# Moving the tail operand and one float32r table to other SBUF addresses in a Fourier-transform and MLP kernel

## The chip, the cores and the metric

The kernel runs on one core of one Trainium2 chip. The metric is device time in microseconds (us) of one execution. Times come from three executions; one further execution was taken with the hardware profiler, and all rows below are from that one.

## The reference

What has to be computed is the real part of a two-dimensional Fourier transform of each of four 3008 x 256 blocks, and then a two-layer perceptron with the SiLU function on the 12032 rows that come out:

```python
batch, seq, dim = (4, 3008, 256)
n_tokens, d_model, d_ff = (12032, 256, 2048)
X = np.fft.fft(x, axis=1)
X = np.fft.fft(X, axis=2)
x = X.real.reshape(B * S, D)
h = x @ w_in
g = h * (1.0 / (1.0 + np.exp(-h)))
return g @ w_out
```

## The kernel before

**Work in chunks.** The transform along the sequence is folded by symmetry until 1506 columns per block are left, in four classes of 376, 378, 376 and 376 columns (`CLASS`, L40). All columns of the four blocks are worked off in 13 chunks (`CHUNKS`, L42): the four classes of block 0 singly, with 376 or 378 columns, then nine chunks of 502 columns. A chunk takes 16 steps, one for each 128 of the 2048 hidden columns.

**A step.** `first` (L443) issues six matmuls, L449 to L451 twice each: the weights `abh` and `abl` (transform along the model axis and `w_in` in one, split into a float32r part and the rest of it) against the chunk's spectrum `uv`, also split. `act` (L459) forms the two signs on VectorE and the SiLU on ScalarE. `second` (L497), three steps later (`LAG`), issues twelve matmuls, four each of L512, L513 and L519, with `w_out` as `woh` and `wol` against the activations `gh` and `gl`, into four accumulators. So a step is 18 matmuls, each with a weight load of 128 x 128 just ahead of it. All these operands are float32r.

**A transform.** Twelve or so steps apart a step also carries the transform of one class of the next block. `turns` (L778 to L784) fixes by hand where: for blocks 1 to 3, with j = 3b + 1, class 0 in chunk j - 1, class 1 in chunk j - 1 too, class 2 in chunk j at step 8, class 3 in chunk j + 1 at step 4. `operand` (L250) prepares `xf` (float32, two buffers in turn) on VectorE, and from the last third of it the tail operand `xh` (float32r, one buffer, L331). `transform` (L339) then issues matmuls on TensorE, with `xf` and `xh` as the stationary operand and the tables as the moving one. For classes 0, 2 and 3 this is twice the same row of seven:

- the tails: one of 376 (or 380) columns (L348) and two of 188 (or 190) columns (L351), `xh` against a float32r table;
- the main part: four of 188 (or 190) columns (L354), `xf` against a float32 table.

Class 0 takes its tables from `t2f` and `t2r`, class 2 from `tef` and `ter`, class 3 from `tof` and `tor`; class 1 uses `tz`, `ter`, `tor`, `tef` and `tof` in 19 matmuls. So class 0 and class 3 issue the same shapes in the same order, and differ by where their operands lie. Behind the transform come the six matmuls of the next step's `first`.

**Addresses.** A pool takes the next free address, and pools lie behind each other in the order in which they are opened: `wts`, `fold`, `raws`, `xs` (with `xf`, `xh` and `wide`), `cp` (`uv`, `ub`), `gh`, `gl`, `mp`, and behind them `wr`, which is closed after the weights are loaded, and in its place `tabs` with the tables (`load_tables`, L615). `place` (L65) puts an empty tile of so many bytes ahead of the next one and thereby moves all that follows.

Of the kernel before, what the change touches and what calls it, by code (L numbers as in the profile page):

```python
# [24 lines left out]
F32 = mybir.dt.float32  # L25
F32R = mybir.dt.float32r
# [24 lines left out]
def fft_mlp(ctx, tc, x1, x2, x2_first, w_in, w_out, te_f, te_r, to_f, to_r, tz_r, t2_f, t2_r, t2f, rot1, rot2, dft, minus_eye, out):  # L51
# [8 lines left out]
    xs = ctx.enter_context(tc.tile_pool(name="xs", bufs=1))  # L60
    cp = ctx.enter_context(tc.tile_pool(name="cp", bufs=3))
# [3 lines left out]
    def place(pool, name, shift):  # L65

        pool.tile([128, shift // 4], F32, name="before_" + name, bufs=1)
# [25 lines left out]
    tabs = {}  # L93
# [461 lines left out]
    late, wr_stack = ctx.enter_context(ExitStack()), ctx.enter_context(ExitStack())  # L555
    wr = wr_stack.enter_context(tc.tile_pool(name="wr", bufs=1))
    ps = late.enter_context(tc.tile_pool(name="ps", bufs=4, space=PSUM))
    place(cp, "uv", 480)
    once = cp.tile([128, 2048], F32, tag="uv", name="once")
    sign, dft_0, dft_1 = once[:, 1790:1792], once[:, 1792:2048], once[:, 0:256]  # L560
    dft_sb = [t.rearrange("p (m k) -> p m k", m=2) for t in (dft_0, dft_1)]
# [53 lines left out]
    def load_tables(q):  # L615
        wr_stack.close()
        pool = ctx.enter_context(tc.tile_pool(name="tabs", bufs=1))
        for name, pair in (("te", (te_f, te_r)), ("to", (to_f, to_r))):
            tabs[name] = [pool.tile([128, t.shape[-1]], d, name=name + x) for t, d, x in zip(pair, (F32, F32R), "fr")]
            for dst, t in zip(tabs[name], pair):  # L620
                nc.gpsimd.dma_start(out=dst, in_=t)
            if name == "te":
                tabs["tz"] = pool.tile([128, 378], F32R, name="tz")
                nc.gpsimd.dma_start(out=tabs["tz"], in_=tz_r)
        tabs["t2"] = pool.tile([128, 376], F32, name="t2f"), wts.tile([128, 1128], F32R, tag="t2", name="t2r")[:, :752]
        for dst, t in zip(tabs["t2"], (t2_f, t2_r)):
            nc.gpsimd.dma_start(out=dst, in_=t)
# [41 lines left out]
    xf = xs.tile([128, 1280], F32, tag="xf", name="xf", bufs=2)  # L669
# [150 lines left out]
    for q, n, m in ((1, 1, 2), (2, 2, 3), (3, 3, 4), (4, 4, 5), (5, 7, 10), (6, 11, 12), (7, 11, 12)):  # L820
        after.setdefault(n - 1 if q < 5 else n, []).append((upper_wo, q))
        fills.setdefault(n + 1, []).append((lower_wo, q))
        if q >= FULL // 2:
            if q > 2:
                fills.setdefault(n - 2 if q == 3 else n - 1, []).append((clear_wo, q))
            mids.setdefault(n + 1, []).append((high_wo, q))
            lows.setdefault(m, []).append((low_wo, q))
    lows[5].append((load_tables, 4))
    after.setdefault(8, []).append((load_wo, 7))
    pace = wts.tile([1, 2], F32, name="pace")  # L830
# [178 lines left out]
```

## Time and profile before

| | |
|---|---|
| median of three executions | 860.05 us (859.88 to 860.71) |
| the profiled execution | 860.15 us |
| its span, first to last instruction | 858.4 us |
| TensorE matmuls busy | 850.9 us, 99% of the span |
| TensorE weight loads busy | 742.7 us, 87% |
| VectorE busy | 719.2 us, 84% |
| ScalarE busy | 511.8 us, 60% |
| GpSimd busy | 167.5 us, 20% |

Matmuls are pipelined, and their ends are modelled: the duration of one is longer than the distance from its start to the next one's, so the distance is what counts. A matmul's busy time alone tells nothing of its speed.

### The profile page before, as it was taken

Reading aid. Unit: us, or ns where it says so; the run is one execution under the profiler, and the core shown is the slowest. Engines: PE = TensorE matmul, PEld = TensorE weight load, DVE = VectorE, ACT = ScalarE, POOL = GpSimd, SP = SyncE. Lnnn points to the kernel's source line nnn. Section 1 sums busy time; section 2 is a strip of 40 time slices with the busy share of each in tenths; the row PEclk is TensorE's granted clock in tenths of the full one; section 3 lists DMA queues with packets and bytes.
Section 4 is the critical chain, followed back from the end, with each engine's and each line's share of the span. In section 5 each row is a group of like instructions: output and inputs, shape, how many; then the busy total and the mean of one; then the engine's idle time right before and its main releaser. Section 6 shows DMA issues by size and latency. Waiting matters only on the chain.

```text
span 858.4 us, 11009 instructions
## 1 busy us (share of the span) xinstructions
PE 850.9 (99%) x4066; PEld 742.7 (87%) x4066; DVE 719.2 (84%) x1074; ACT 511.8 (60%) x648; POOL 167.5 (20%) x239
## 2 busy tenths in 40 slices
PE   8999999999999999999999999999999999999998
PEld 6799999999988888888888888888888888888886
DVE  5899999999898987989789978889878887777773
ACT  5767856565656565566565556457656556545454
POOL 4757541323040401305013000502000000000000
PEclk9999999999999999999999999999999999999999
DMA  9755454073341516035034203404021011201001
GB/s 322 265 152 78 111 82 89 2 122 32 53 93 5 103 49 105 4 21 135 1 59 97 11 1 56 100 0 58 1 10 48 4 7 49 10 1 49 1 0 49
DMA packets 24182, 52.12 MB, mean 61 GB/s; under 512 B 3728, under 2 KB 13072, under 8 KB 24128
## 3 DMA queue, kind: packets, MB, share of 16 engines
q1 hardware_dynamic: 19888, 38.21, 21.2%
q0 software_dynamic: 4240, 13.21, 8.6%
q8 instruction: 32, 0.52, 0.3%
q14 instruction: 22, 0.18, 0.1%
HBM read 36.17 MB, written 12.34 MB: 57 GB/s over the span
## 4 chain that ended last, share of the span: by engine, by line
PE 97%; DMA 2%; DVE 0%; ACT 0%; SPq 0%; issue 0%; ACTq 0%
PE acc L513 20%; PE acc L519 20%; PE acc L512 20%; PE pq L449 10%; PE pq L451 10%; PE pq L450 10%; PE pq L354 3%; DMA win<-in_w_in_dram 2%; PE pq L351 1%; PE acc L510 1%; PE pq L348 1%; ACT wf L82 0%; PE pq L676 0%; PE pw L588 0%; DVE wf L86 0%; SPq L78 0%
## 5 line engine op out<-in xcount | busy, mean ns | idle before, releaser
L480 ACT ACTIVATE h<-h 128x1004 f32<-128x1004 f32 (+3 forms) x208 | 202.5, 974 | 281.5 <-DVE h L465 278.5
L513 PE MATMUL acc<-g,wol 128*128 128x502 f32 (+2 forms) x824 | 307.5, 373 | 0.0
L512 PE MATMUL acc<-g,woh 128*128 128x502 f32 (+2 forms) x824 | 307.2, 373 | 0.0
L495 DVE TENSOR_TENSOR g<-h,g 128x1004 fp32r<-128x1004 f32 (+3 forms) x208 | 240.8, 1159 | 14.1 <-ACT g L483 13.0
L519 PE MATMUL acc<-g,woh 128*128 128x502 f32 (+2 forms) x824 | 213.5, 373 | 0.0
L483 ACT ACTIVATE g<-h 128x1004 fp32r<-128x1004 f32 (+3 forms) x208 | 202.7, 975 | 7.2 <-PE acc L513 0.9
L463 DVE SCALAR_TENSOR_TENSOR p<-ub,a,pq 128x502 f32<-128x502 f32 (+2 forms) x208 | 144.7, 695 | 73.4 <-PE pq L451 69.7
L513 PEld LDWEIGHTS acc<-g,wol 128*128 128x128 f32 x824 | 155.6, 189 | 22.1
L512 PEld LDWEIGHTS acc<-g,woh 128*128 128x128 f32 x824 | 155.7, 189 | 21.8
L519 PEld LDWEIGHTS acc<-g,woh 128*128 128x128 f32 x824 | 153.1, 189 | 21.8
L449 PE MATMUL pq<-uv,abh 128*128 128x502 f32 (+2 forms) x416 | 158.0, 380 | 0.0
L451 PE MATMUL pq<-uv,abl 128*128 128x502 f32 (+2 forms) x416 | 155.1, 373 | 0.0
L450 PE MATMUL pq<-uv,abh 128*128 128x502 f32 (+2 forms) x416 | 154.9, 372 | 0.0
L464 DVE TENSOR_TENSOR h<-p,pq 128x502 f32<-128x502 f32 (+2 forms) x208 | 132.8, 638 | 22.1 <-DVE p L463 0.5
L465 DVE TENSOR_TENSOR h<-p,pq 128x502 f32<-128x502 f32 (+2 forms) x208 | 131.2, 631 | 0.0
L449 PEld LDWEIGHTS pq<-uv,abh 128*128 128x128 f32 x416 | 78.6, 189 | 11.2 <-issue 0.2
L451 PEld LDWEIGHTS pq<-uv,abl 128*128 128x128 f32 x416 | 78.5, 189 | 10.9
L450 PEld LDWEIGHTS pq<-uv,abh 128*128 128x128 f32 x416 | 78.6, 189 | 10.6
L150 POOL DMA_DIRECT2D raw<-in_x_dram x22 | 19.1, 882 | 222.1 <-DMA raw<-in_x_dram 221.0
L234 POOL TENSOR_TENSOR ri<-ri,raw 128x256 f32<-128x256 f32 x24 | 22.7, 953 | 135.4 <-ACT ri L229 134.9
L528 ACT ACTIVATE o<-acc 128x502 f32<-128x502 f32 (+2 forms) x52 | 28.0, 558 | 16.4 <-PE acc L519 14.0
L218 POOL TENSOR_TENSOR raw<-raw 128x512 f32<-128x512 f32 x12 | 16.2, 1348 | 18.5 <-DMA raw<-in_x_dram 18.5
(140 smaller groups left out, 471.2 us busy)
## 6 DMA issues: line engine op xcount, KB each, us to landing
raw<-in_x_dram SPq DMA_DIRECT2D x22, 512.0 KB, 8.4
raw<-in_x_dram POOLq DMA_DIRECT2D x20, 512.0 KB, 7.4
out_dram<-o SPq DMA_DIRECT2D x36, 251.0 KB, 2.1
win<-in_w_in_dram SPq DMA_DIRECT2D x8, 512.0 KB, 8.5
wo<-in_w_out_dram SPq DMA_DIRECT2D x8, 512.0 KB, 8.8
out_dram<-o SPq DMA_DIRECT2D x12, 188.0 KB, 4.2
ub<-wide SPq DMA_DIRECT2D x8, 188.0 KB, 8.7
x_t<-in_x_first_dram SPq DMA_DIRECT2D x2, 512.0 KB, 9.5
```

The source lines that it names most:

```text
L449: nc.tensor.matmul(po, abh[:, i, fs], uvh[:, i, :n], start=True, stop=False)
L450: nc.tensor.matmul(po, abh[:, i, fs], uvl[:, i, :n], start=False, stop=False)
L451: nc.tensor.matmul(po, abl[:, i, fs], uvh[:, i, :n], start=False, stop=True)
L463: stt(p[:, :n], ub[:, :n], a128[f // 2][:, f % 2:f % 2 + 1], pq[0][:, :n], op0=ALU.mult, op1=ALU.add)
L464: tt(h[:, 0, :n], p[:, :n], pq[1][:, :n], op=ALU.add)
L465: tt(h[:, 1, :n], p[:, :n], pq[1][:, :n], op=ALU.subtract)
L480: nc.scalar.activation(h[:, sg, :n], h[:, sg, :n], AF.Silu)
L483: nc.scalar.activation(gh[:, sg, :n], h[:, sg, :n], AF.Copy)
L495: tt(gl[:, sg, :n], g[:, sg, :n], gh[:, sg, :n].bitcast(F32), op=ALU.subtract)
L512: nc.tensor.matmul(po, wo[0][f // 2][:, f % 2, es], gh[:, sg, :n], start=f == 0, stop=False)
L513: nc.tensor.matmul(po, wo[1][f // 2][:, f % 2, es], gh[:, sg, :n], start=False, stop=False)
L519: nc.tensor.matmul(accs[c][i][:, :n], wo[0][f // 2][:, f % 2, es], gl[:, sg, :n], start=False, stop=f == NF - 1)
```

## The change

An empty tile of 448 bytes per partition is put ahead of `xf`, and the one ahead of `uv` shrinks from 480 to 32 bytes, so that `uv` and all pools behind it stay where they are. An empty tile of 320 bytes is put ahead of `tor` in the pool of the tables. Every engine has the same instructions in the same order with the same waits as before; only addresses differ.

```diff
-    place(cp, "uv", 480)
+    place(xs, "xf", 448)
+    place(cp, "uv", 32)
     once = cp.tile([128, 2048], F32, tag="uv", name="once")
...
         for name, pair in (("te", (te_f, te_r)), ("to", (to_f, to_r))):
-            tabs[name] = [pool.tile([128, t.shape[-1]], d, name=name + x) for t, d, x in zip(pair, (F32, F32R), "fr")]
+            tabs[name] = []
+            for t, d, x in zip(pair, (F32, F32R), "fr"):
+                if name + x == "tor":
+                    place(pool, "tor", 320)
+                tabs[name].append(pool.tile([128, t.shape[-1]], d, name=name + x))
             for dst, t in zip(tabs[name], pair):
                 nc.gpsimd.dma_start(out=dst, in_=t)
```

Byte addresses within a partition, as allocated, with the rest that is left on division by 512:

| tile | type, use on TensorE | before | rest | after | rest |
|---|---|---|---|---|---|
| `xf`, two buffers | float32, stationary | 120000, 125120 | 192 | 120448, 125568 | 128 |
| `xh` | float32r, stationary | 130240 | 192 | 130688 | 128 |
| `wide` | not read by TensorE | 134368 | 224 | 134816 | 160 |
| `tor` | float32r, moving | 218432 | 320 | 218752 | 128 |
| `t2f` | float32, moving | 221440 | 256 | 221760 | 64 |
| `tef` | float32, moving | 209280 | 384 | the same | 384 |
| `ter` | float32r, moving | 211584 | 128 | the same | 128 |
| `tz` | float32r, moving | 214624 | 96 | the same | 96 |
| `tof` | float32, moving | 216160 | 96 | the same | 96 |
| `t2r` | float32r, moving | 84608 | 128 | the same | 128 |
| `abh`, `abl`, `woh`, `wol` | float32r, stationary | from 16512 | 128 | the same | 128 |
| `uv`, `gh`, `gl` | float32r, moving | from 137856 | 128 | the same | 128 |

All slices of 128 columns that become stationary start a multiple of 512 bytes behind their tile's start, so they keep the tile's rest.

## Rows read from the trace of the kernel before

**Rows 1.** The page's parts 1 and 2: busy time by engine, and TensorE's granted clock
```profile
PE 850.9 (99%) x4066; PEld 742.7 (87%) x4066; DVE 719.2 (84%) x1074; ACT 511.8 (60%) x648; POOL 167.5 (20%) x239
...
PEclk9999999999999999999999999999999999999999
```

**Rows 2.** The page's part 4: the chain that ended last, by engine
```profile
PE 97%; DMA 2%; DVE 0%; ACT 0%; SPq 0%; issue 0%; ACTq 0%
```

**Rows 3.** The chain in order of time, behind class 3: start us, length us, what
```profile
331.49 0.93 PE acc L519 x4
...
335.69 0.93 PE acc L519 x4
```

**Rows 4.** The same view, behind class 2
```profile
292.92 0.89 PE acc L519 x4
...
296.94 0.89 PE acc L519 x4
```

**Rows 5.** Stretches from transform to transform: us, PE busy (instructions), clock, DMA share, GB/s
```profile
323.73:374.26 50.53, 50.53 (x219) 1.00 0.30 46
528.03:578.56 50.53, 50.53 (x218) 1.00 0.29 46
732.34:858.40 126.06, 122.09 (x524) 0.99 0.09 19
...
376.19:424.57 48.38, 48.38 (x219) 1.00 0.38 69
427.39:475.77 48.38, 48.38 (x219) 1.00 0.36 69
477.71:526.10 48.39, 48.39 (x219) 1.00 0.17 26
```

**Rows 6.** Line L519 behind the first and the third class 3: ns min/median/max, first and last start
```profile
L519 PEld LDWEIGHTS acc<-g,woh x48: 192/192/192, 326.9 to 373.8; 128*128 128x128 f32 x48
L519 PE MATMUL acc<-g,woh x48: 396/396/397, 327.1 to 374.0; 128*128 128x502 f32 x48
...
L519 PE MATMUL acc<-g,woh x119: 396/396/396, 735.7 to 853.3; 128*128 128x502 f32 x119
```

**Rows 7.** The same line behind class 0
```profile
L519 PEld LDWEIGHTS acc<-g,woh x48: 187/188/188, 379.2 to 424.1; 128*128 128x128 f32 x48
L519 PE MATMUL acc<-g,woh x48: 382/385/389, 379.5 to 424.3; 128*128 128x502 f32 x48
```

**Rows 8.** TensorE in order of time, second half of a class 3 transform and behind it
```profile
323.00 0.37 PE L351 MATMUL pq<-tor,xh 128*128 128x188 f32 x2
...
324.09 0.39 PE L450 MATMUL pq<-uv,abh 128*128 128x502 f32 x1
324.32 0.40 PE L451 MATMUL pq<-uv,abl 128*128 128x502 f32 x1
```

**Rows 9.** The same view, second half of a class 0 transform and behind it
```profile
375.46 0.36 PE L351 MATMUL pq<-t2r,xh 128*128 128x188 f32 x2
...
376.55 0.39 PE L450 MATMUL pq<-uv,abh 128*128 128x502 f32 x1
376.77 0.39 PE L451 MATMUL pq<-uv,abl 128*128 128x502 f32 x1
```

**Rows 10.** Lines L351 and L354 over the whole span: durations min/median/max in ns
```profile
L351 PE MATMUL pq<-tor,xh x20: 248/272/279, 63.0 to 731.7; 128*128 128x188 f32 x20
...
L354 PE MATMUL pq<-tof,xf x64: 322/323/348, 63.4 to 732.3; 128*128 128x188 f32 x64
...
L354 PE MATMUL pq<-t2f,xf x24: 322/323/348, 195.0 to 580.5; 128*128 128x188 f32 x24
```

**Rows 11.** The chain in order of time, a chunk of 376 columns behind class 3
```profile
181.61 0.69 PE acc L519 x4
184.73 0.69 PE acc L519 x4
```

## The prediction

> **What bounds the kernel now.** The page's busy times come first. TensorE's matmuls fill 99% of the span, and the granted clock stands at full speed in every slice [rows 1], which is the upper of its two levels, 2.4 GHz. The chain that ended last is 97% TensorE [rows 2], so hardly any wait of another engine is in it: the time is the number of matmuls times the distance between them. Only a change of that distance, or of a transform's own length, can move the result.
>
> So the distance is the next thing to read. The chain in order of time shows the four L519 matmuls that close each step. Behind class 3 they come 4.20 us apart (331.49 to 335.69) [rows 3], behind class 2 4.02 us apart (292.92 to 296.94) [rows 4]. Both are steps of 18 matmuls of 502 columns with the same lines and, since buffers only rotate, the same kinds of addresses. That is 233.3 ns per matmul against 223.3 ns, or **10.0 ns** between a slow and a fast rhythm.
>
> The stretches from one transform to the next show that the rhythm belongs to the class that went before [rows 5]. Twelve steps take 50.53 us behind class 3, both times, and 48.38 or 48.39 us behind classes 0, 1 and 2. The clock reads 1.00 in all of these. Single matmuls tell the same: L519 takes 396 ns and its load 192 ns behind the first class 3, 396 ns also from 735.7 us to the end behind the third [rows 6], and 385 and 188 ns behind class 0 [rows 7]. Load and matmul grow together, which looks like two reads that get in each other's way, and the state holds until the next transform. This reading is an inference; that there are two rhythms is a measurement.
>
> **What sets the rhythm.** It is there at once. Behind class 3, the step's first L450 starts 0.23 us before its L451 (324.09 to 324.32) [rows 8]; behind class 0 it is 0.22 us (376.55 to 376.77) [rows 9]. Nothing waits there. The two transforms have the same shapes in the same order, so what differs is the addresses of their operands and the rhythm in which they were entered. I take it that some nanoseconds in when the last matmul of the transform ends choose the rhythm. The tail pair with `tor` lasts 0.37 us [rows 8], the one with `t2r` 0.36 us [rows 9], so the tails do differ by about that much. The main part does not: 322/323/348 ns with `tof` and with `t2f` [rows 10].
>
> **The change, part by part.**
>
> *Class 3 leaves its transform in the fast rhythm.* After the change `xh` and `tor` have the rest 128, as `t2r` has had and keeps, so that the tails of class 3 stand to each other as those of class 0 do. If class 3 then ends as class 0 does, three stretches change. The first two give 50.53 - 48.38 = 2.15 us each [rows 5]. In the third, 27 `first` parts of 6 matmuls and 30 `second` parts of 12 are left (11 steps of chunk 11, 16 of chunk 12, and the lag of three), 522 matmuls; at 10.0 ns each that is 5.22 us. Sum: 2.15 + 2.15 + 5.22 = **9.52 us**. The cover of the faster rhythm is there: VectorE is busy 84% of the span [rows 1] and already keeps up with the fast stretches between.
>
> *The tails themselves.* 26 half transforms carry a pair of L351 behind an L348 (22 of classes 0, 2 and 3, and 4 of class 1). No row shows these matmuls at the new addresses. Bounds come from the ends of the L351 group, 248 and 279 ns [rows 10]: 31 ns for each of 26 pairs, 0.81 us gained or lost. I take zero, because the pairs differ by 0.01 us between tables now [rows 8, 9], and keep both ends.
>
> *The main part.* `xf` and `t2f` move too. With two tables at rests 96 and 256 the L354 rows agree to the nanosecond [rows 10], so this costs nothing.
>
> *Everything else.* ScalarE, VectorE and GpSimd touch `xf`, `xh` and `wide` at new addresses, and six table loads land as before. No row compares such an operation at two addresses. ScalarE at 60% and GpSimd at 20% [rows 1] have slack to cover it, and the order written by hand prepares a transform's operands ahead of its step; if the cover failed, a transform would wait, and no such wait stands in the chain now. The parts of 376 and 378 columns keep their rhythm: 3.12 us a step behind a class 3 transform (181.61 to 184.73) [rows 11], 173 ns per matmul, with no slower state in the rows.
>
> Sum against the profiled execution: 860.15 - 9.52 = 850.63, so **850.6 us**. That execution lies 0.10 us above the median of 860.05.
>
> **A rule of the Trainium skill against it.** The distance in a fast stretch is 223.3 ns and in a slow one 233.3 ns, with the clock at 1.00 [rows 3 to 5]. The Trainium skill, page "TensorE: Matmul & The Clock Gate", section "Step-by-step: what each phase is for", says that moving data and weight loads have separate read ports, so a load takes nothing from the running matmul; its section "Back-to-back issue gap" gives columns / 2.4 + 2.5 ns, by which 502 columns would take 211.7 ns, an estimate. By that rule addresses would not matter and the sum would be zero. The trace does not agree with it: both rhythms are longer, and loads lengthen with the matmuls [rows 6, 7].
>
> **The rivals.**
>
> *No change.* The shifts may leave every transform ending as it does, because where the end falls was set by shapes and by the rhythm before. For it: the L354 rows do not care for addresses [rows 10], and class 0 comes after a slow stretch and class 3 after a fast one, so history could explain the difference between them without any address. Against it: the tail pairs differ by 0.01 us [rows 8, 9]. Time: 860.1 us. The separate ports of the skill's page lead here too. Chance 0.18.
>
> *Class 3 is freed, another class falls.* `xh` moves for all classes and `tor` is read by class 1 as well, so all four ends may shift. A fall costs 2.15 us for each 12-step stretch [rows 5]: class 0 or class 1 has two behind it, 4.30 us, giving 850.6 + 4.3 = 854.9; class 2 has three, 6.45 us, giving 857.1. Chance 0.19.
>
> *Slower: the slow entry spreads.* If a common rest of tail operand and table is what leads into the slow rhythm, every class ends as class 3 does now. The place is the first L449 behind each transform, and it decides there: L450 to L451 at 0.23 us instead of 0.22. Class 3 gains nothing, classes 0, 1 and 2 pay 4.30 + 4.30 + 6.45 = 15.05 us: 875.2 us. In part, with class 2 alone joining class 3, it is 866.6 us. For it: nothing yet shows that equal rests are the good case, and three entries of four are good now. Against it: class 2 already reads its table at 128, and is fast. Chance 0.17.
>
> **How the numbers follow.** The forecast has the rest, 0.46. A measurement of this kernel can tell about 0.2%, or 1.7 us, from no change. Faster is the forecast and the second rival, 0.65; same is 0.18; slower is 0.17. The range of the forecast alone is 849.8 to 851.4 by the bound on the tails. The range for 8 in 10 starts a little under that, at 849.6, and reaches over the second rival and no change to the edge of "same", 862.0, leaving out the slow case of 0.17.
>
> **What would show it.** Right: the stretch behind the first class 3 lasts 48.4 us, L519 there takes 385 ns with loads of 188 ns, and the end of the program comes at steps of 4.02 us. Wrong: a stretch of 50.5 us behind any class; which class tells the rival. Wrong in its ground would be a 502-column step at neither 4.02 nor 4.20 us, or a wait of TensorE ahead of L348.

## The result, and the profile after

The changed kernel takes 850.92 us (median of four executions, 850.74 to 851.59) against 860.21 us for the kernel before on the same chips: a ratio of 0.9893, with a 95% interval from 0.9878 to 0.9908. The forecast was 850.6 us. The profiled execution took 850.74 us with a span of 849.0 us, 9.4 us less than the profiled one of before (860.15 and 858.4 us).

The page's part 1 of the changed kernel, which answers to [rows 1]:

```profile
PE 842.0 (99%) x4066; PEld 738.9 (87%) x4066; DVE 715.8 (84%) x1074; ACT 511.8 (60%) x648; POOL 168.6 (20%) x239
```

TensorE's matmuls are busy 8.9 us less with the same number of instructions, and its weight loads 3.8 us less; VectorE, ScalarE and GpSimd have the same number of instructions as before and busy times within 3.4 us of it. The stretches from one transform to the next, in the columns of [rows 5] (us, PE busy with its instructions, granted clock, DMA share, GB/s): the first three lie behind class 3, the others behind classes 0, 1 and 2.

```profile
323.73:372.12 48.39, 48.39 (x219) 1.00 0.30 48
525.91:574.29 48.38, 48.38 (x218) 1.00 0.30 48
728.08:849.00 120.92, 116.88 (x524) 0.99 0.10 19
374.04:422.43 48.39, 48.39 (x218) 1.00 0.38 69
425.25:473.64 48.39, 48.39 (x218) 1.00 0.36 69
475.59:523.97 48.38, 48.38 (x218) 1.00 0.17 26
```

The three stretches behind class 3 lost 2.14, 2.15 and 5.14 us, together 9.43 us, and that is the whole difference: the stretches behind the other classes are as before to 0.01 us each, and the clock column reads as it did. The chain in order of time behind the first class 3 (start us, length us, what) now has steps of 4.02 us (331.18 to 335.20), where [rows 3] had 4.20 us:

```profile
331.18 0.89 PE acc L519 x4
335.20 0.89 PE acc L519 x4
```

L519 behind the first and the third class 3 (durations min/median/max in ns, first and last start), which answers to [rows 6]: matmuls of 385 instead of 396 ns, loads of 188 instead of 192 ns, up to the end of the program.

```profile
L519 PEld LDWEIGHTS acc<-g,woh x48: 187/188/188, 326.8 to 371.7; 128*128 128x128 f32 x48
L519 PE MATMUL acc<-g,woh x48: 382/385/389, 327.0 to 371.9; 128*128 128x502 f32 x48
...
L519 PE MATMUL acc<-g,woh x120: 382/385/389, 731.3 to 844.6; 128*128 128x502 f32 x120
```

So the slow rhythm is gone behind class 3 and came up nowhere else. What is not said by this is why: whether the new rests as such do it, or only the shift of some nanoseconds that they give.

### The profile page after: what moved, and what is told of

It is laid out like the page before. It is cut to its first block, busy times and chain, and to the rows that moved or that the text cites. A ratio compares the mean times of both kernels' runs of the same rounds, so it can differ in the third digit from the quotient of the medians.

```text
span 849.0 us, 11009 instructions
## 1 busy us (share of the span) xinstructions
PE 842.0 (99%) x4066; PEld 738.9 (87%) x4066; DVE 715.8 (84%) x1074; ACT 511.8 (60%) x648; POOL 168.6 (20%) x239
## 4 chain that ended last, share of the span: by engine, by line
PE 96%; DMA 2%; DVE 0%; ACT 0%; SPq 0%; issue 0%; ACTq 0%
PE acc L513 20%; PE acc L519 20%; PE acc L512 20%; PE pq L449 10%; PE pq L450 10%; PE pq L451 10%; PE pq L354 3%; DMA win<-in_w_in_dram 2%; PE pq L351 1%; PE acc L510 1%; PE pq L348 1%; ACT wf L82 0%; PE pq L681 0%; PE pw L589 0%; DVE wf L86 0%; SPq L78 0%
## 5 line engine op out<-in xcount | busy, mean ns | idle before, releaser
L519 PE MATMUL acc<-g,woh 128*128 128x502 f32 (+2 forms) x824 | 211.3, 370 | 0.0
L519 PEld LDWEIGHTS acc<-g,woh 128*128 128x128 f32 x824 | 152.0, 188 | 20.6
L451 PE MATMUL pq<-uv,abl 128*128 128x502 f32 (+2 forms) x416 | 154.0, 370 | 0.0
L450 PE MATMUL pq<-uv,abh 128*128 128x502 f32 (+2 forms) x416 | 153.8, 370 | 0.0
L451 PEld LDWEIGHTS pq<-uv,abl 128*128 128x128 f32 x416 | 78.1, 188 | 10.4
L450 PEld LDWEIGHTS pq<-uv,abh 128*128 128x128 f32 x416 | 78.1, 188 | 10.0
```

The lines of the kernel that those rows point to most:

```text
L450: nc.tensor.matmul(po, abh[:, i, fs], uvl[:, i, :n], start=False, stop=False)
L451: nc.tensor.matmul(po, abl[:, i, fs], uvh[:, i, :n], start=False, stop=True)
L519: nc.tensor.matmul(accs[c][i][:, :n], wo[0][f // 2][:, f % 2, es], gl[:, sg, :n], start=False, stop=f == NF - 1)
```

## The experiments

Three theories were on trial. **A**: the instant at which a transform's last matmul ends picks the rhythm, and addresses act only by moving it. **B**: tail operand and table need equal rests, or the rest 128. **C**: nothing special, any shift of any operand moves the ends, and a class falls slow by chance.

### Which of the two moves does it

The table alone (with `t2f`, which lies behind it), the tail operand alone (with `xf` and `wide`, which move with it), and the table alone moved to the rest that `xh` has in the kernel before (192). The diffs are against the kernel before; lines that only spell out the loop over the tables are left out.

```diff
# e1_tor_alone
...
+                if name + x == "tor":
+                    place(pool, "tor", 320)
...
# e2_xh_alone
-    place(cp, "uv", 480)
+    place(xs, "xf", 448)
+    place(cp, "uv", 32)
# e5_tor_192
...
+                if name + x == "tor":
+                    place(pool, "tor", 384)
...
```

> Only the table tor moves (rest 128, and t2f behind it to rest 64); xf and xh stay at rest 192. Theory A (the instant at which a transform's last matmul ends, taken on a short repeating grid of some 13 ns, chooses the rhythm; addresses act only through a few ns in the tails): class 3's tails now relate to each other as those of class 0 did before, so its end shifts by some ns off the point that was slow; the three stretches behind class 3 go to 48.4 us for 12 steps and the time to about 850.7 us; class 1, which reads tor in its tails too, keeps 48.4. Theory B (tail operand and table must have the same rest): 192 and 128 are not the same, class 3 stays slow at 50.5 us and the time at 860 us. Theory C (chance; any shift of any operand moves the ends and each class falls fast or slow by its own): no number, some class may be slow.

> Only xf, xh and wide move (rest 128); tor stays at rest 320 and t2f at 256. Theory A: the ends of all classes shift by some ns; class 3 leaves the slow point with them if its tails take another length, 850.7 us, else 860 us; classes 0 and 2, whose operands stand here as in the changed kernel apart from t2f, are fast as there. Theory B (same rest needed): 128 and 320 are not the same, class 3 stays slow, 860 us. With e1 fast and e2 slow the table does it; with both fast either shift is enough; with both slow the two are needed together.

> The kernel before with tor alone moved, to rest 192, the rest that xf and xh have there (t2f behind it at 128). Theory B in the form that equal rests of tail operand and table are the good case: fast behind class 3. In the form that it has to be 128: slow, 860 us. Theory A: nothing is special in equal rests; the tails take another few ns and class 3 is fast unless its end falls on the slow instant again, which is about one in eight: 850.7 us.

Measured: 850.41 us with the table alone (ratio 0.9884, 0.9868 to 0.9901), 851.01 us with the operand alone (ratio 0.9895, 0.988 to 0.991), 850.64 us in one execution with the table at 192. The chain in order of time behind the first class 3 shows 4.02 us a step in each; here of the first, then of the second, then of the third kernel:

```profile
327.22 0.89 PE acc L519 x4
331.24 0.89 PE acc L519 x4
```

```profile
327.98 0.89 PE acc L519 x4
332.00 0.89 PE acc L519 x4
```

```profile
327.05 0.89 PE acc L519 x4
331.07 0.89 PE acc L519 x4
```

What follows: either move is enough, and they do not add. Rests of operand and table may be equal or not (192 and 128, 128 and 320, 192 and 192, in these three runs), and all are fast; 192 and 320, in the kernel before, is the slow pair. Theory B falls in both its forms. These runs do not tell A from C.

### The rhythm without any change of address

To move the end of the transform without moving an address, the last matmul of class 3 that the program writes got fewer columns (the second call of L354 in the second half); part of the sum is left out in those columns. In the trace each call of L354 stands as two matmuls, and the cut shortens both. With 16 columns less, behind the second class 3 of e6_before_cut_period, two of the eight have 172 columns instead of 188, and the shortest takes 309 ns instead of 322:

```profile
L354 PE MATMUL pq<-tof,xf x8: 309/322/347, 525.9 to 527.4; 128*128 128x188 f32 x6, 128*128 128x172 f32 x2
```

A column takes about 0.86 ns in one of them: the chain of before has 16 such matmuls of 188 or 190 columns in 2.59 us. So a column less moves the end by twice that, some 1.7 ns, and the expectations that count 0.8 ns a column, here and in the next section, have their shifts at half the size.

```diff
# e3_before_cut: {7: 3, 11: 6, 15: 12}
# e6_before_cut_period: {7: 8, 11: 16, 15: 4}
# e9_before_cut_near: {7: 1, 11: 2, 15: 7}
...
                 for g, (p, q) in enumerate(cuts):
+                    q -= {7: 3, 11: 6, 15: 12}.get(c, 0) * i * g
                     main(dst[:, p:q], 256 * g + 128 * i, f[:, p:q], stop=g == 1)
```

> The kernel before, all addresses as they were; the last matmul of the class 3 transform is 3, 6 and 12 columns shorter in blocks 1, 2 and 3 (those columns of the output miss a part of their sum), so that it ends 2.5, 5 and 10 ns earlier. Theory A (the instant of the end decides): before, it ended at 6.7 to 7.3 on a grid of 13.3 ns and was slow, while ends at 0.3 to 6.3 and at 10.7 were fast; now it ends at about 4.2, 2.0 and 10.7, so all three stretches are fast, 48.4 us for 12 steps, and the time is near 850.7 us. Theory B (addresses decide by themselves): all three stay slow, 860.1 us.

> The kernel before, all addresses as they were; the last matmul of the class 3 transform is 8, 16 and 4 columns shorter in blocks 1, 2 and 3 (those columns of the output miss a part of their sum). In the traces so far the starts of the 502-column matmuls of any one run fall on a grid of 6.67 ns, which is 8 columns of this matmul. Theory A (the instant of the end on that grid decides): 8 and 16 columns move the end by one and two whole periods, so the stretches behind the first and the second class 3 are slow as before, 50.5 us for 12 steps, although 3, 6 and 12 columns had made all of them fast; 4 columns are half a period, and the last stretch is fast. Time about 855.5 us. Theory A' (the end only has to leave one narrow instant, with no period): all fast, 850.7 us. Theory B (addresses by themselves): ruled out by the run with 3, 6 and 12 columns unless all three are slow again.

> The kernel before with the last matmul of the class 3 transform shorter by 1, 2 and 7 columns in blocks 1, 2 and 3 (those columns of the output miss a part of their sum): 0.8, 1.7 and 5.8 ns earlier. So far 0, 8 and 16 columns were slow and 3, 4, 6 and 12 fast. It asks how wide the slow window in the period of 8 columns is. Theory A with a narrow window (about one column): all three fast, 850.7 us. With a window of up to three columns: 1 and 7, next to 0 and 8, are slow too, and 2 is fast: the first and the third stretch slow, 858 us.

Measured, one execution each: 850.78 us with 3, 6 and 12 columns less, 854.38 us with 8, 16 and 4, 849.97 us with 1, 2 and 7. The chain of the first of them, behind its first class 3 (the added line makes the old L519 L520), 4.02 us a step:

```profile
327.26 0.89 PE acc L520 x4
331.28 0.89 PE acc L520 x4
```

The chain of the second, behind the first class 3 (8 columns less) and the second (16 less), 4.20 or 4.21 us a step, and behind the third (4 less), 4.02 us:

```profile
330.90 0.93 PE acc L520 x4
335.11 0.93 PE acc L520 x4
...
530.98 0.93 PE acc L520 x4
535.18 0.93 PE acc L520 x4
...
739.18 0.89 PE acc L520 x4
743.20 0.89 PE acc L520 x4
```

Its stretches from class 3 to the next transform, in the columns of [rows 5], are those of before, 50.53 us, to 0.03 us:

```profile
323.79:374.31 50.52, 50.52 (x220) 1.00 0.30 46
527.90:578.40 50.50, 50.50 (x220) 1.00 0.29 46
```

And the third kernel behind its first class 3, one column less than before:

```profile
330.49 0.89 PE acc L520 x4
334.51 0.89 PE acc L520 x4
```

What follows: with all addresses as before, 0, 8 and 16 columns less are slow, and 1, 2, 3, 4, 6, 7 and 12 are fast; each number other than 0 was tried once, behind one of the three class 3 transforms. The slow rhythm comes back after 8 columns, and one column to either side of 0 and 8 ends it. In time, by two cycles of 2.4 GHz (0.83 ns) for each column in each of the two matmuls, close to the 0.86 ns above, 8 columns are 13.3 ns and one column is 1.7 ns. The step lengths fit such a period: two slow matmuls of 4.20 / 18 = 233.3 ns are 35 times that, four of the fast rhythm at 4.02 / 18 = 223.3 ns, whose starts repeat their distances after four (223, 222, 229 and 220 ns), 67 times, and one of 376 columns with 3.12 / 18 = 173.3 ns 13 times. That is an agreement of numbers, not a test, and the 4.10 us a step further down (17.1 times for one matmul) does not share it.

At the addresses of before, then, nothing but columns of one call makes the slow rhythm and ends it, with no address moved, as theory A has it. Two things are argued and not shown. The cut changes the size of two matmuls as well as the instant at which they end, and 8 columns are also 32 bytes of float32; no run moved the end with all sizes and addresses kept. And that the changed kernel is fast because its end left that instant is inferred from these runs; the end of its transform was not brought back onto it. For moved addresses the runs do not tell A from C.

### Making the slow rhythm with the new addresses

The same cut in the changed kernel, to bring its class 3 onto the slow instant.

```diff
# e4_after_cut: {7: 7, 11: 5, 15: 7}
# e7_after_cut_less: {7: 6, 11: 7, 15: 5}
# e10_after_cut_rest: {7: 4, 11: 3, 15: 2}
...
                 for g, (p, q) in enumerate(cuts):
+                    q -= {7: 7, 11: 5, 15: 7}.get(c, 0) * i * g
                     main(dst[:, p:q], 256 * g + 128 * i, f[:, p:q], stop=g == 1)
```

> The changed kernel, all addresses as in it; the last matmul of the class 3 transform is 7, 5 and 7 columns shorter in blocks 1, 2 and 3 (those columns of the output miss a part of their sum), so that it ends 5.8, 4.2 and 5.8 ns earlier. Theory A: it ended at 12.7, 11.3 and 13.0 on a grid of 13.3 ns and was fast; now it ends at 6.8, 7.2 and 7.2, where the kernel before was slow, so the slow rhythm is back behind class 3, 50.5 us for 12 steps, and the time is near 860 us although the addresses are those of the faster kernel. Theory B: stays fast, 850.9 us or a few ns less.

> The changed kernel with the last matmul of the class 3 transform shorter by 6, 7 and 5 columns in blocks 1, 2 and 3 (those columns of the output miss a part of their sum). With 7, 5 and 7 columns no slow stretch came; the ends then lay, as far as 1 ns tells, about 1, 6 and 1 columns short of the slow instant on the 6.67 ns grid of that run. Theory A: one column less (6), two more (7) and two less (5) bring the ends onto or just past that instant, so at least one stretch behind class 3 is slow, 50.5 us, with the addresses of the faster kernel. If none is slow, the slow instant cannot be hit from the ends as the trace gives them, and theory A holds only for leaving it.

> The changed kernel with the last matmul of the class 3 transform shorter by 4, 3 and 2 columns in blocks 1, 2 and 3 (those columns of the output miss a part of their sum). 0, 5, 6 and 7 columns gave no slow stretch. Theory A with one window for all kernels: the window is somewhere in the period of 8 columns, so if it is as wide as a column one of these three or of the untried 1 hits it, and one stretch behind class 3 is slow (50.5 us for 12 steps). If all are fast, the instant of the end alone does not make the slow rhythm with the new addresses; it is then one of at least two conditions, and the addresses of the tails carry the other.

Measured, one execution each: 850.37, 851.63 and 850.88 us. No stretch is slow. The chain of the last one behind its first class 3, 4.02 us a step:

```profile
327.35 0.89 PE acc L520 x4
331.37 0.89 PE acc L520 x4
```

What follows: three misses. The first rested on ends read on a grid from the start of each trace, and that grid is not the same from run to run; and it took a column for half of the time by which it moves the end, as the second did. So these sizes were not aimed, and what counts is which of the eight values of the period were covered. Over the three blocks 0 and 2 to 7 columns were tried and only 1 was not, but any one block saw only four of the eight values. So it stays open whether the slow instant was passed by, or the addresses of the tails carry a second condition that the new ones do not meet. By what was put on record ahead of the last run, three fast stretches there speak for the second. Columns alone end the slow rhythm and bring it back at the old addresses; that it can be reached at the new ones is not shown.

### The fast rhythm itself

The last three runs move the moving operands (`uv`, `gh`, `gl` and the tables but `t2r`) against the weights, which stay at rest 128. Diffs are against the changed kernel.

```diff
# e8_moving_192
-    place(cp, "uv", 32)
+    place(cp, "uv", 96)
# e11_moving_384
-    place(cp, "uv", 32)
+    place(cp, "uv", 288)
# e12_moving_160
-    place(cp, "uv", 32)
+    place(cp, "uv", 64)
```

> The changed kernel with uv, the activations gh and gl and the tables 64 bytes further (rest 192), while all weights stay at 128. It asks whether the fast rhythm itself, 223.3 ns per matmul, hangs on how moving and stationary addresses stand to each other. If it does not, steps stay at 4.02 us and the time within 850 to 860 us, each class fast or slow by its end. If it does, steps take another length in all stretches: anything from 3.81 us (18 matmuls of 211.7 ns) to 4.3 us, the time from 820 to 875 us.

> The changed kernel with uv, gh, gl and the tables 256 bytes further (rest 384), all weights at 128. With 64 bytes further the steps of 376 columns took 3.07 us instead of 3.12 and those of 502 columns 4.08 instead of 4.02. It asks whether another distance between moving and stationary addresses is better for the 502 columns. If only the distance within 128 bytes counts (64 was the other half), this kernel reads like the changed one, 4.02 and 3.12 us, about 851 us. If the distance within 512 bytes counts, both step lengths are new; below 4.02 us a step it beats both kernels.

> As the run before, with 32 bytes further (rest 160). If distances of a part of 64 bytes count at all, steps differ from 4.02 and 3.12 us; if only whole pieces of 64 bytes count, they stay, and the time is about 851 us, each class fast or slow by its end.

Measured, one execution each: 857.34 us with 64 bytes, 851.6 us with 256, 862.49 us with 32. The chain of the first, in chunk 2 (376 columns) and behind the second class 3 (502 columns): 3.07 and 4.08 us a step instead of 3.12 and 4.02.

```profile
150.86 0.68 PE acc L519 x4
153.93 0.68 PE acc L519 x4
...
531.42 0.91 PE acc L519 x4
535.50 0.91 PE acc L519 x4
```

The chain of the third, at the same chunk and behind the first class 3: 3.12 and 4.10 us.

```profile
151.23 0.69 PE acc L519 x4
154.35 0.69 PE acc L519 x4
...
328.57 0.91 PE acc L519 x4
332.67 0.91 PE acc L519 x4
```

With 256 bytes the steps are those of the changed kernel, 3.12 and 4.02 us. So the addresses of the moving operands do set the length of a fast step, 256 bytes further counts as nothing, and the place that the kernel has is the best of those tried for 502 columns, not for 376. Whether it is their distance to the weights that counts is not shown: no run moved the weights. None of the three beats the changed kernel, since 144 of its 208 steps have 502 columns.

## Why the prediction was right

**The bound.** TensorE's chain was the time, and a gain in the distance of its matmuls came through in full: 9.43 us in the three stretches, 9.4 us in the span, 9.41 us in the profiled time. The cover that was named held; VectorE reads 84% as before.

**Class 3.** The terms were 2.15, 2.15 and 5.22 us; they measured 2.14, 2.15 and 5.14 us. The last one is 0.08 us short of the count. Its matmuls are not: TensorE's busy time there went from 122.09 [rows 5] to 116.88 us, 5.21 of the 5.22 us. The rest lies behind the last matmul, where the stretch goes on for 3.97 us before and 4.04 us now, some of it the rounding of the span's end.

**The ground given for it was wrong in part.** The prediction chose the forecast because tail operand and table of class 3 would stand to each other as those of class 0 do. The runs with one of the moves alone, and the one at rest 192, are fast without that. The 0.01 us between the tail pairs, from which it took that the tails differ, is no sign either: in the second class 3 of the kernel before, as slow as the first, the pair lasts 0.36 us as with `t2r`.

```profile
527.30 0.36 PE L351 MATMUL pq<-tor,xh 128*128 128x188 f32 x2
```

Nor did the change make class 3's transform shorter or longer. By the starts in the kept traces, to the nanosecond, it takes 1933, 1934 and 1934 ns from its first matmul to the first one behind it in the kernel before, and 1933 ns three times in the changed one; the transform of class 2 ahead of it went from 1949 or 1950 to 1954 ns, that of class 0 from 1935 to 1926. With the table alone moved class 3 takes 1927 to 1930 ns. So if it is the instant of the end that freed class 3 in the changed kernel, it moved with the instant at which the transform starts, and not through its own tails; no run settles it.

What carries the forecast is the other sentence, that some nanoseconds in the end of the transform choose the rhythm; the runs with fewer columns at the old addresses speak for it. The rest 128 was thus no aimed hit, and that no other class fell was luck in part. Seven of the nine cuts at the old addresses gave 4.02 us a step, and the other two were whole periods; if every class at every set of addresses is slow with one chance in eight, an estimate from these cuts, class 3 is freed with 0.88, where the prediction's forecast and second rival have 0.65 together, and all four classes are fast with 0.59, where the forecast has 0.46.

**The sign "it is there at once" does not decide.** Behind class 3 itself the changed kernel starts as the kernel before did: L450 to L451 takes 0.23 us, at the same 324.09 and 324.32 us as in [rows 8], and yet the stretch is a fast one with 48.39 us. Behind class 1 it is the same (425.62 to 425.85, then 48.39 us). TensorE in order of time, behind class 3 and behind class 1:

```profile
324.09 0.39 PE L450 MATMUL pq<-uv,abh 128*128 128x502 f32 x1
324.32 0.39 PE L451 MATMUL pq<-uv,abl 128*128 128x502 f32 x1
324.54 0.39 PE L449 MATMUL pq<-uv,abh 128*128 128x502 f32 x1
...
425.25 0.53 PE L449 MATMUL pq<-uv,abh 128*128 128x502 f32 x1
425.62 0.39 PE L450 MATMUL pq<-uv,abh 128*128 128x502 f32 x1
425.85 0.39 PE L451 MATMUL pq<-uv,abl 128*128 128x502 f32 x1
426.07 0.39 PE L449 MATMUL pq<-uv,abh 128*128 128x502 f32 x1
```

In both the next matmul follows after 0.22 us, so the first distance does not tell the rhythm that the stream settles in. Only the stretch tells.

**The tails and the main part** cost nothing that the time shows, as taken. The L351 group with `tor`, 248/272/279 ns in [rows 10], is 247/273/279 ns now:

```profile
L351 PE MATMUL pq<-tor,xh x20: 247/273/279, 62.8 to 727.4; 128*128 128x188 f32 x20
```

**The rivals.** *No change* fell: class 3 is fast. History is not needed to explain class 3 either, because in the runs with 3 columns and with 1 column less its first transform is entered as before and is left fast. *Another class falls* did not come. Over the kernel before, the changed one and the three runs with other addresses of operand and table, one class of 20 is slow, class 3 of the kernel before; that the others have a chance near one in eight, as the cuts have it for class 3, is an estimate that no run tested. *The slow entry spreads* rested on equal rests as the bad case; at 128 and 128, and at 192 and 192, they are fast.

**The rule that spoke against it.** The Trainium skill, page "TensorE: Matmul & The Clock Gate", section "Step-by-step: what each phase is for", holds that a weight load takes nothing from the running matmul. What the prediction took from it, that addresses would not matter, does not hold here: with the moving operands 64 bytes further the same matmuls go from 4.02 to 4.08 us a step in 502 columns and from 3.12 to 3.07 us in 376, by addresses alone. Whether the loads have a part in that, no run shows: every matmul of these streams has its load, and none was taken away. The section "Back-to-back issue gap" of the same page of the Trainium skill gives columns / 2.4 + 2.5 ns for a matmul by itself, not for a stream with a load ahead of each; so 223.3 against the estimate of 211.7 ns, which the prediction held against the rule, decides nothing about it.

## What to carry to other kernels

Where TensorE is the bound, compare the distance of equal matmuls between stretches before looking for waits: two rhythms of the same work, with the clock at full speed, can hide a per cent that no idle time shows. When a shift of addresses removes a slow rhythm, move something that has nothing to do with addresses by the same few nanoseconds as well; here one column less in one call did for its stretch what the change did, so the good address was not a rule to build on. In this kernel the rhythm was set anew behind each transform, and 8 columns less there brought the slow one back, so an edit near such a break is a reason to read the stretch again.

## What the runs showed that was not expected

- A stream of matmuls of 502 columns has two steady rhythms, 223.3 and 233.3 ns, at equal addresses and equal clock, and keeps the one it got, in the last stretch for 522 matmuls, to the end of the program.
- At the addresses of before, which one it gets turns on the columns of the last call ahead of it, to within one column (some 1.7 ns of the end) and with a period of 8 columns (13.3 ns): 0, 8 and 16 columns less are slow, seven other values are fast.
- Moving the moving operands by 64 bytes changes the distance by 60 / 18 = 3.3 ns for 502 columns, for the worse, and by 50 / 18 = 2.8 ns for 376, for the better; by 256 bytes it changes nothing.
